# Linear attention and a GELU MLP on one core: the second weight cast by GpSimd's DMAs, and three changes of order

## The chip, the core and the metric

One core of a Trainium2 chip runs the whole program. The time is that of the device in microseconds, from a kernel that is launched once; smaller is better. Three runs of the kernel before took 264.68, 264.91 and 265.53 us.

The core has TensorE (PE in the profile; PEld is its loading of weights), VectorE (DVE), ScalarE (ACT), GpSimd (POOL), and SyncE (SP), which here only issues DMAs. Sixteen DMA engines move the data.

## What is computed

Eight batches, eight heads, 576 positions, 64 values per head, all in float32:

```python
q_s = exp(q - max(q, -1)); q_s /= sum(q_s, -1)        # over the 64 values
k_s = exp(k - max(k, 2));  k_s /= sum(k_s, 2)         # over the 576 positions
kv  = einsum('bhsd,bhse->bhde', k_s, v)
x   = einsum('bhsd,bhde->bhse', q_s, kv)              # to 4608 rows of 512
h   = x @ w_in                                        # 512 x 2048
g   = 0.5 * h * (1 + erf(h / sqrt(2)))
out = g @ w_out                                       # 2048 x 512
```

## The kernel before

The program is written in order by hand for each engine: an engine does its instructions in the order of the code, and semaphores make it wait for the others. Nothing is reordered behind the author's back.

**Chunks.** The 4608 rows are nine chunks of 512: chunk c (0 to 7) is the first 512 positions of batch c, and chunk 8 is the 64 left over of each batch. For a batch, ACT takes exponentials of q (`exp_q`) and k (`exp_k`), DVE sums q's over the 64 values (`q_sums`), DVE or GpSimd scales them (`q_scale`, `norm_q`), v is cast to bf16 (`cast_v`), PE makes k'v (`kv_mm`), DVE divides it (`kv_norm`). The scaled q is transposed: on PE for batches 0 and 1 (`tp_mm`, `tp_quarters`), by a transposing DMA from SP for the later ones (`xbar_step`). PE then makes x (`x_mm`), which DVE and ACT copy out of PSUM (`x_evac`).

**The two large products.** Chunk 0's are plain: `h_phase` does h in 16 tiles t of 128 hidden units, in groups, with GELU on ACT, and `y_mm` sums the 16 tiles into four banks. Chunk 1's h is plain too (`h_pairs`). From chunk 1's output product (`y_phase`) on, and from chunk 2's h (`h_waves`) on, the products are done in Strassen's way, with seven products of half size in place of eight. The seven are numbered 1 to 7 in the calls `mm(1, ...)` to `mm(7, ...)`, and each needs sums of operands: `quad_weights` makes those of w_in (four DVE operations for each of two sets, `sums0` and `sums`), `mix_wo` those of w_out (in `w16`, `w7` and in place), `x_sums` those of x, `s_parts` those of g (into `s5`, `s12` and in place). In `y_phase` the order is 1, 5, 6, 2, 7, 3, 4; bank `pa` takes products 1, 6, 7 and 4, where 6 and 7 are added onto what is there, so what is there must have been copied out first. `after(i)` calls what `ins` has for product i: the work of later batches that is to stand there in the engines' orders. `y_last` does chunk 8's output product in two halves j, each with three banks of its own, and stores each piece as it is done.

**Banks.** PSUM has eight banks. `roles` says which bank has which task in a chunk, and `turn_roles` permutes them from chunk to chunk. In `h_waves` the argument `mid` is set for chunk 2 alone, where the order of the wave is another one.

**Weights.** w_in comes by ten SP DMAs into float32 tiles `wi` (tags w0 to w4), in five blocks of 256, 256, 512, 512 and 512 columns. `cast_wi` and `cast_wi_dm` make bf16 of it in `wi_bf`, where a block of n columns is read with stride n/128: hidden unit m of tile c is column m n/128 + c. w_out comes by further SP DMAs (`load_wo`, `load_wo_row`) in the same order of rows, 4 or 8 KB in a row per partition, and DVE and ACT cast it (`cast_wo`) into `wo_bf`. On SP the loads stand in this order: q, k, v of batch 0, w_in, three quarters of w_out, then q, k and v of batch 1 with the rest of w_out between them, then batch 2 (`load(2)`). `wst` is the pool of those weight tiles; a tile of the same tag waits until the one before it is read: `quad_s` of `sums0` takes w4 and `w16` takes w0.

Of the kernel before, what the change touches and what calls it, by code (L numbers as in the profile page):

```python
# [8 lines left out]
FP32 = mybir.dt.float32  # L9
# [7 lines left out]
def kernel(  # L17
# [122 lines left out]
    def load(b):  # L140
        load_main(b, "q", q)
        load_pair(b, "k", k)
        load_pair(b, "v", v)
# [289 lines left out]

    def quad_weights(w):

        q = quad["s"][w] = wst.tile([128, 4, 2, 512], BF16, tag=("w4", "w1")[w], name="quad_s")
        up, dn = slice(w * 512, w * 512 + 512), slice((w + 2) * 512, (w + 3) * 512)
        a11, a12 = wi_bf[:, 0:2, up], wi_bf[:, 2:4, up]
        a21, a22 = wi_bf[:, 0:2, dn], wi_bf[:, 2:4, dn]
        s1, s2, s3, s4 = (q[:, i] for i in range(4))  # L440
        return [
            lambda: tt(s1, a21, a22), lambda: tt(s2, s1, a11, ALU.subtract),
            lambda: tt(s3, a11, a21, ALU.subtract), lambda: tt(s4, a12, s2, ALU.subtract),
        ]
# [13 lines left out]
    def turn_roles():  # L458

        r = dict(roles)  # L460
        roles.update(bb=r["x3"], ba=r["kv1"], x0=r["bb"], x1=r["kv0"], x2=r["x0"], x3=r["ba"],
                     kv0=r["x1"], kv1=r["x2"])

    def h_waves(c, mid):
# [144 lines left out]
        s_parts(c, 0, 4, (2, 3, 4) if mid else (3, 4))  # L609
        s_parts(c, 4, 4, (1, 2, 3, 4))  # L610
        turn_roles()

    def h_phase(c, ins, groups={}, banks={}, t1=0):

# [54 lines left out]
    def y_phase(c, ins):  # L669

        act, wgt = y_operands(c)
        at = {"ya": 2, "yb": 0, "yc": 3} if c == 1 else {"ya": roles["ba"], "yb": roles["bb"], "yc": roles["x0"]}
        pa, pb, pc = (bank(at[n], n) for n in ("ya", "yb", "yc"))
        ysb = [moe_sb.tile([128, 2, DM], FP32, tag="y_sb", name="y_sb", bufs=2) for i in range(2)]
        c11, c12 = ysb[0][:, :, 0:HN], ysb[0][:, :, HN:DM]
        c21, c22 = ysb[1][:, :, 0:HN], ysb[1][:, :, HN:DM]

        def two(ps):
            return ps.rearrange("p (j n) -> p j n", j=2)

        def mm(m, ps, first):
            for j in range(2):
                for k in range(HK):
                    nc.tensor.matmul(  # L684
                        ps[:, j * HN:(j + 1) * HN], act[m][:, k, j * 128:(j + 1) * 128],
                        wgt[m][:, k, :], start=(first and k == 0 and j == 0),
                        stop=(k == HK - 1), skip_group_check=True,
                    )

        def after(i):  # L690
            for fn in ins.get(i, []):
                fn()

        mm(1, pa, True)
        nc.scalar.copy(out=c11, in_=two(pa))  # L695
        after(1)
        mm(5, pb, True)
        nc.vector.tensor_copy(out=c22, in_=two(pb))
        after(5)
        mm(6, pa, False)  # L700
        tt(two(pb), two(pa), c22)
        after(6)
        mm(2, pc, True)
        tt(c11, c11, two(pc))
        after(2)
        mm(7, pa, False)
        tt(c22, two(pa), c22)
        after(7)
        mm(3, pb, False)
        nc.scalar.copy(out=c12, in_=two(pb))  # L710
        y_store(c, 0, ysb[0])
        after(3)
        mm(4, pa, False)
        nc.scalar.copy(out=c21, in_=two(pa))
        y_store(c, 1, ysb[1])
        after(4)

    def y_last(c):
# [16 lines left out]
        def mm(j, m, ps, first, n=slice(0, HN)):  # L735
            for k in range(HK):
                nc.tensor.matmul(  # L737
                    ps[:, n], act[m][:, k, j * 128:(j + 1) * 128], wgt[m][:, k, n],
                    start=(first and k == 0), stop=(k == HK - 1), skip_group_check=True,
                )  # L740

        for j in range(2):
            pa, pb, pc = banks[j]
            c11, c12 = ysb[0][:, j, 0:HN], ysb[0][:, j, HN:DM]
            c21, c22 = ysb[1][:, j, 0:HN], ysb[1][:, j, HN:DM]
            mm(j, 1, pa, True)
            nc.scalar.copy(out=c11, in_=pa)
            if j:
                store(0, 0, HN, both, (0,))
                store(1, 0, 0, both, (0,))  # L750
            mm(j, 5, pb, True)
            nc.scalar.copy(out=c22, in_=pb)
            mm(j, 6, pa, False)
            tt(pb, pa, c22)
# [35 lines left out]
        return w  # L790


    def cast_wi(i, w, eng):
        n = wi_cols[i]
        r = n // 128
        o = wi_bf[:, :, wi_off[i]:wi_off[i] + n].rearrange("p d (c m) -> p d c m", c=r)
        w = w[:, :, 0:n].rearrange("p d (m c) -> p d c m", c=r)
        if eng == "pv":

            nc.gpsimd.tensor_copy(out=o[:, 0:2], in_=w[:, 0:2])  # L800
            nc.vector.tensor_copy(out=o[:, 2:4], in_=w[:, 2:4])
        else:
            for c in range(NDM):
                nc.vector.tensor_copy(out=o[:, c], in_=w[:, c])  # L804

    def cast_wi_dm(i, w, dm, eng):

        n = wi_cols[i]
        r = n // 128
        o = wi_bf[:, dm, wi_off[i]:wi_off[i] + n].rearrange("p (c m) -> p c m", c=r)  # L810
        w = w[:, dm, 0:n].rearrange("p (m c) -> p c m", c=r)
        eng.tensor_copy(out=o, in_=w)

    def load_wo(i):
        w = wst.tile([128, 4, DM], FP32, tag=f"w{i}", name="w")
        src = moe_w_out[i * 512:(i + 1) * 512, :]
        if i == 0:
            for h in range(2):
                nc.sync.dma_start(
                    out=w[:, 2 * h:2 * h + 2],  # L820
                    in_=src[256 * h:256 * h + 256].rearrange("(p c) f -> p c f", c=2),
                )
            return w
        src = src.rearrange("(p c) f -> p c f", c=4)
        if i == 3:
            nc.sync.dma_start(out=w[:, 0:2], in_=src[:, 0:2])
            return w
        nc.sync.dma_start(out=w, in_=src)
        return w

    def load_wo_row(w, c):
        src = moe_w_out[3 * 512:4 * 512, :].rearrange("(p c) f -> p c f", c=4)
        nc.sync.dma_start(out=w[:, c], in_=src[:, c])

    def cast_wo(i, w, c0=0, n=4, eng="v"):
        o, w = wo_bf[:, 4 * i + c0:4 * i + c0 + n, :], w[:, c0:c0 + n]
        if eng == "v":
            nc.vector.tensor_copy(out=o, in_=w)
        else:
            nc.scalar.copy(out=o, in_=w)  # L840

    w16 = None

# [23 lines left out]


    touch = singles.tile([16, 3, 2], FP32)
    for i, a in enumerate((v[0].rearrange("h (p n) d -> (h p) (n d)", n=NS)[0:128:8, 0:2],  # L870
                           moe_w_in[0:128:8, 0:2], moe_w_out[0:512:32, 0:2])):
        nc.scalar.dma_start(out=touch[:, i, :], in_=a)

    load_pair(0, "v", v, 4)
    wi = [load_wi(i) for i in range(5)]
    wo = [load_wo(i) for i in range(3)]
    load_main(1, "q", q, 2)
    load_k1(0)
    wo.append(load_wo(3))
    load_k1(1)  # L880
    for hp in range(2):
        load_v1(hp)
    load_wo_row(wo[3], 2)
    load_wo_row(wo[3], 3)
    load_v1(2)
    load_v1(3)
    load(2)
    nc.vector.memset(zeros32, 0.0)
    setup_tiles()
    warm(7, zeros32)  # L890
# [20 lines left out]
    kv_mm(0, 1)  # L911
    kv_norm(0, 1)
    for dm in range(NDM):
        cast_wi_dm(0, wi[0], dm, nc.gpsimd)
    x_tile(0, 3, psum_h, "h")
    x_mm(0, 0)
    x_evac(0, 0, "s")
# [1 line left out]
    x_mm(0, 1)  # L919
    x_evac(0, 2, "s")  # L920
    x_evac(0, 3)
    cast_wi(1, wi[1], "pv")
    table(AF.Gelu)

    def ybank():
# [1 line left out]

    sums0 = quad_weights(0)
    h_phase(0, {
        0: [lambda: cast_wi(2, wi[2], "v")],  # L930
        2: [lambda: cast_wi(3, wi[3], "v")],
        6: [lambda: cast_wi(4, wi[4], "v")],
        9: sums0[0:2] + [lambda: cast_wo(0, wo[0])],
        15: [lambda: cast_wo(1, wo[1], eng="s")],
    }, groups={0: 2, 4: 4, 8: 4}, banks={
        3: ybank, 6: ybank, 8: ybank,
        9: lambda: psum_a.tile([128, M], FP32, tag="a", name="ps"),
# [3 lines left out]

    exp_q(1, parts=2)
    exp_k(1, parts=2, part=0)
    cast_wo(3, wo[3], 0, 1, "s")
    cast_wo(3, wo[3], 1, 1, "s")
    exp_k(1, parts=2, part=1)
    table(AF.Gelu)
    w16 = wst.tile([128, 2, HK, HN], BF16, tag="w0", name="w16")
    sums = quad_weights(1)
    for fn in sums0[2:]:  # L950
        fn()
    cast_wo(2, wo[2])
    for m in (3, 2, 4):
        mix_wo(m, 0)
    tps = [psum.tile([128, HP, J, 64], BF16, tag=f"k{i}", name="tp") for i in (5, 1)]
# [11 lines left out]
        y_part(t, range(J))  # L967
    load(3)
    mix_wo(1, 0)
    cast_wo(3, wo[3], 2, 1)  # L970
    cast_wo(3, wo[3], 3, 1)
    y_part(12, range(J))
    y_part(13, range(J))
    tp_quarters(1, tps)
# [37 lines left out]
    for m in (3, 2, 4, 1):  # L1012
# [1 line left out]
    quad["r"] = wst.tile([128, 4, 2, HT], FP32, tag="w2", name="r")  # L1014
    quad["t"] = wst.tile([128, 4, 2, HT], BF16, tag="w3", name="quad_t")
    h1 = {p + 3: [lambda p=p: cast_v(2, p, nc.scalar)] for p in range(HP)}
    h1[1] = [sums[0]]
    h1[3] += sums[1:3]
    h_pairs(1, h1, done=t1s, turn=Banks(2, 0, 5, 6))

# [3 lines left out]

    y_phase(1, {
        1: [sums[3], lambda: norm_q(2, 0, 2)],
        5: [lambda: norm_q(2, 1, 2, nc.vector)],
        6: [lambda: cast_v_all(3), lambda: xbar_step(2), lambda: exp_q(3)],
        2: [lambda: kv_step(2), lambda: exp_k(3), lambda: q_sums(3)],
        3: [lambda: table(AF.Gelu)],  # L1030
        4: [lambda: load(4), lambda: x_all(2, (3, 4, 1, 5)),
            lambda: kv_step(3, lambda: x_sums(2, (1,))), lambda: x_sums(2, (2,))],
# [73 lines left out]
```

## Time and profile before

| what | value |
|---|---|
| median of three runs | 264.91 us (264.68 to 265.53) |
| the profiled execution | 264.49 us, of which 262.4 us are its span, from first to last instruction |
| mean granted TensorE clock | 0.993 |
| bytes moved by DMA | 50.23 MB, mean 191 GB/s |
| ACT busy in the span | 190.1 us |
| DVE busy in the span | 190.0 us |
| POOL busy in the span | 54.5 us |

A line of a group or of the timeline names line, engine, operation and tiles (out<-in). Idle time stands with what ended it: `[3.26 <-ACT y_sb L695]` is 3.26 us in which the engine waited, ended by that copy on ACT. In a list of waits a line reads: who waited <- for whom: microseconds in total, times, the longest. A clock of 0.50 is half of the full TensorE clock.

### The profile page before, as it was taken

To read this page: it belongs to the slowest core of one execution; us is meant where nothing else is said; L and a number is where in the kernel's file an instruction comes from. 1 tells how busy PE (TensorE), PEld (TensorE's weight loads), DVE (VectorE), ACT (ScalarE), POOL (GpSimd) and SP (SyncE) were. 2 spreads that over 40 slices of the span, in tenths; PEclk is the share of its full clock that TensorE was granted. 3 is DMA by queue.
4 is the path that set the end of the run, shared out by engine and by line. 5 is a ranking of instruction groups with operands and counts; after the bars stand their busy time and mean duration, and the time that the engine had idled before them with its cause. 6 is when DMAs were issued, how large, how long until landed. Compare 5 with 4: busy or idle time off the path is not lost.

```text
span 262.4 us, 6525 instructions
## 1 busy us (share of the span) xinstructions
PE 251.1 (96%) x2678; PEld 196.9 (75%) x2678; DVE 190.0 (72%) x336; ACT 190.1 (72%) x324; POOL 54.5 (21%) x85
## 2 busy tenths in 40 slices
PE   7999999995999899999999999999999999999993
PEld 3544444444778788888888888888888888888783
DVE  1878699778468778687868886887688679548922
ACT  4876887799556986789688958895888587068721
POOL 1520033003404136004700470047000700000000
PEclk9999999999799999999999999999999999999999
DMA  7999999991319998880787079402700250040033
GB/s 241 400 381 424 402 406 399 397 418 61 82 80 319 327 308 315 204 318 1 260 231 273 6 258 223 99 2 78 166 4 0 82 160 2 0 162 2 0 80 84
DMA packets 43166, 50.23 MB, mean 191 GB/s; under 512 B 20224, under 2 KB 30464, under 8 KB 42880
## 3 DMA queue, kind: packets, MB, share of 16 engines
q1 hardware_dynamic: 42416, 49.13, 55.3%
q10 hardware_dynamic: 720, 0.69, 1.0%
q8 instruction: 21, 0.34, 0.6%
q14 instruction: 9, 0.07, 0.1%
HBM read 36.70 MB, written 9.44 MB: 176 GB/s over the span
## 4 chain that ended last, share of the span: by engine, by line
PE 73%; DMA 12%; ACT 7%; DVE 4%; issue 1%; POOL 1%; ACTq 1%; SPq 0%; DVEq 0%
PE ya L684 18%; PE qa L498 16%; PE yb L684 8%; PE qb L498 8%; DMA w<-in_moe_w_in_dram 6%; PE ps L387 5%; PE yc L684 5%; PE qc L498 4%; DMA f<-in_v_dram 4%; ACT g L522 3%; PE ya L737 2%; DMA touch<-in_moe_w_out_dram 2%; PE kv L225 2%; PE ps L353 2%; PE yb L737 1%
## 5 line engine op out<-in xcount | busy, mean ns | idle before, releaser
L684 PEld LDWEIGHTS <-g 128*128 128x128 bf16 x448 | 43.3, 98 | 7.9 <-issue 2.2
L498 PEld LDWEIGHTS <-quad_s 128*128 128x128 bf16 x448 | 43.8, 98 | 5.1
L684 PEld LDWEIGHTS <-s 128*128 128x128 bf16 x336 | 33.6, 100 | 7.9 <-issue 3.4
L498 PEld LDWEIGHTS <-wi_bf 128*128 128x128 bf16 x336 | 32.8, 98 | 3.8
L278 POOL TENSOR_TENSOR e<-e,recq 128x256 bf16<-128x256 bf16 x40 | 24.3, 644 | 31.3 <-DVE recq L264 21.0
L498 PE MATMUL qa<-quad_t,quad_s 128*128 128x256 bf16 x224 | 29.2, 273 | 0.0
L430 DVE TENSOR_TENSOR qb<-qa,r 128x512 f32<-128x512 f32 x28 | 18.2, 694 | 14.1 <-PE qa L498 9.6
L387 PE MATMUL ps<-xT,wi_bf 128*128 128x512 bf16 x128 | 28.2, 379 | 0.0
L684 PE MATMUL ya<-w,g 128*128 128x256 bf16 x224 | 26.8, 273 | 0.6 <-DVE y_sb L430 0.6
L684 PE MATMUL yb<-wo_bf,s 128*128 128x256 bf16 x224 | 26.7, 273 | 0.0
L263 DVE TENSOR_REDUCE qsum<-e 128x16 f32<-128x1024 bf16 (+1 forms) x12 | 20.9, 1738 | 5.6 <-ACT e L173 5.6
L387 PEld LDWEIGHTS <-wi_bf 128*128 128x128 bf16 x128 | 12.3, 98 | 15.3 <-DVE wi_bf L804 0.6
L393 ACT ACTIVATE g<-ps 128x512 bf16<-128x512 f32 x32 | 17.6, 601 | 6.2 <-PE ps L387 5.8
L173 ACT ACTIVATE e<-f 128x512 bf16<-128x512 f32 (+1 forms) x42 | 20.5, 557 | 1.9 <-DMA f<-in_q_dram 1.5
L522 ACT ACTIVATE g<-r 128x512 bf16<-128x512 f32 x28 | 17.3, 631 | 6.1 <-DVE r L430 6.1
L522 ACT ACTIVATE g<-qc 128x512 bf16<-128x512 f32 x28 | 15.2, 594 | 7.4 <-PE qc L498 7.4
L710 ACT COPY y_sb<-yb 128x512 f32<-128x512 f32 x7 | 4.1, 587 | 21.4 <-PE yb L684 21.4
L269 POOL TENSOR_TENSOR e<-e,recq 128x1024 bf16<-128x1024 bf16 (+1 forms) x4 | 9.3, 2332 | 48.8 <-DVE recq L264 48.8
L378 DVE CAST xT<-ps 128x512 bf16<-128x512 f32 x18 | 11.7, 687 | 10.0 <-PE ps L353 8.4
L430 DVE TENSOR_TENSOR r<-qa,r 128x512 f32<-128x512 f32 x28 | 18.0, 684 | 1.0 <-PE qa L498 0.7
L684 PE MATMUL ya<-w,s 128*128 128x256 bf16 x112 | 15.0, 292 | 3.3 <-ACT y_sb L695 3.3
L190 POOL CAST v_aug<-f 128x576 bf16<-128x576 f32 x25 | 17.5, 738 | 2.5 <-DMA f<-in_v_dram 2.4
(95 smaller groups left out, 447.9 us busy)
## 6 DMA issues: line engine op xcount, KB each, us to landing
out_dram<-y_sb SPq DMA_DIRECT2D x16, 512.0 KB, 3.7
f<-in_k_dram SPq DMA_DIRECT2D x6, 1152.0 KB, 9.9
f<-in_v_dram SPq DMA_DIRECT2D x6, 1152.0 KB, 9.2
f<-in_q_dram SPq DMA_DIRECT2D x6, 1024.0 KB, 7.2
w<-in_moe_w_in_dram SPq DMA_DIRECT2D x6, 512.0 KB, 9.2
f<-in_v_dram SPq DMA_DIRECT2D x8, 288.0 KB, 6.2
f<-in_q_dram SPq DMA_DIRECT2D x4, 512.0 KB, 8.9
w<-in_moe_w_out_dram SPq DMA_DIRECT2D x2, 1024.0 KB, 11.8
```

The lines of the kernel that those rows point to most:

```text
L173: nc.scalar.activation(out=dst[:, i], in_=src[:, u], func=AF.Exp)
L190: eng.tensor_copy(out=o, in_=i)
L263: nc.vector.reduce_sum(out=qsum, in_=st[b]["eq"][:, :, i * w:(i + 1) * w, :], axis=AX.X)
L269: eng.tensor_tensor(out=e, in0=e, in1=st[b]["recq"].unsqueeze(3).to_broadcast([128, J, w, D]), op=ALU.mult,)
L278: nc.gpsimd.tensor_tensor(out=e, in0=e, op=ALU.mult, in1=st[b]["recq"][:, j, i:i + 4].unsqueeze(2).to_broadcast([128, 4, D]),)
L378: nc.vector.tensor_copy(out=st[b]["xT"][:, hp, :], in_=ps)
L387: nc.tensor.matmul(ps, wi_bf[:, dm, t * 128:(t + 1) * 128], st[c]["xT"][:, dm, :], start=(dm == 0), stop=(dm == NDM - 1),)
L393: nc.scalar.activation(out=st[c]["g"][:, t, :], in_=ps, func=AF.Gelu)
L430: eng.tensor_tensor(out=out, in0=in0, in1=in1, op=op)
L498: nc.tensor.matmul(held[kind, q][:, u], w, mov[m][:, k], start=(m in (1, 5) and u == 0 and k == 0), stop=(k == 1), skip_group_check=True,)
L522: nc.scalar.activation(out=g[:, t:t + 2, half], in_=held[kind, q], func=AF.Gelu)
L684: nc.tensor.matmul(ps[:, j * HN:(j + 1) * HN], act[m][:, k, j * 128:(j + 1) * 128], wgt[m][:, k, :], start=(first and k == 0 and j == 0), ...
```

## The change

It does five things.

1. In chunk 1's `y_phase` the copy of product 1 is DVE's, not ACT's; the second half of q's norm for batch 2 stands after product 6's sum, not after product 5's copy; the sum over e of batch 3 stands after product 7's sum, not after `kv_step(2)`.
2. After chunk 2's wave two banks change places in `roles`.
3. `y_last` does product 1 of both halves first.
4. w_in's columns lie in plain order in `wi_bf`, and the casts read without a stride, four of a quarter and then two of a half for each block. The sums of w_in's sets (`sums0`, `sums`) move forward in DVE's order, and two weight tiles change tags.
5. w_out comes by four GpSimd DMAs, each of four tiles (512 rows of 2 KB), float32 in memory and bf16 in `wo_bf`; the casts on DVE and ACT go. GpSimd issues them after a copy of one column that waits for the first half of w_in's last block. SP issues a DMA of 16 values of `wo_bf` tile 7, which waits for the second of the four, and behind it the loads of batch 1 and 2.

```diff
@@ quad_weights
-        q = quad["s"][w] = wst.tile([128, 4, 2, 512], BF16, tag=("w4", "w1")[w], name="quad_s")
+        q = quad["s"][w] = wst.tile([128, 4, 2, 512], BF16, tag=("w0", "w1")[w], name="quad_s")
@@ h_waves
         turn_roles()
+        if mid:
+            roles.update(ba=roles["x2"], x2=roles["ba"])
@@ y_phase
-        nc.scalar.copy(out=c11, in_=two(pa))
+        (nc.vector.tensor_copy if c == 1 else nc.scalar.copy)(out=c11, in_=two(pa))
@@ y_last
         for j in range(2):
+            mm(j, 1, banks[j][0], True)
+            nc.scalar.copy(out=ysb[0][:, j, 0:HN], in_=banks[j][0])
+        for j in range(2):
...
-            mm(j, 1, pa, True)
-            nc.scalar.copy(out=c11, in_=pa)
+            mm(j, 5, pb, True)
             if j:
                 store(0, 0, HN, both, (0,))
                 store(1, 0, 0, both, (0,))
-            mm(j, 5, pb, True)
@@ weights
-    def cast_wi(i, w, eng):
...
-    def cast_wo(i, w, c0=0, n=4, eng="v"):
...
+    def cast_wi(i, w, eng, d0=0, n=1):
+
+        c = slice(wi_off[i], wi_off[i] + wi_cols[i])
+        eng.tensor_copy(out=wi_bf[:, d0:d0 + n, c], in_=w[:, d0:d0 + n, 0:wi_cols[i]])
+
+    def load_wo(t, n=4):
+
+        nc.gpsimd.dma_start(
+            out=wo_bf[:, t:t + n, :],
+            in_=moe_w_out[t * 128:(t + n) * 128, :].rearrange("(t p) f -> p t f", p=128),
+        )
@@ the start
+    landed = singles.tile([16, 2], BF16)
...
-    wo = [load_wo(i) for i in range(3)]
-    load_main(1, "q", q, 2)
-    load_k1(0)
-    wo.append(load_wo(3))
-    load_k1(1)
-    for hp in range(2):
-        load_v1(hp)
-    load_wo_row(wo[3], 2)
-    load_wo_row(wo[3], 3)
-    load_v1(2)
-    load_v1(3)
-    load(2)
...
-    cast_wi(1, wi[1], "pv")
+    cast_wi(1, wi[1], nc.gpsimd, 0, 2)
+    cast_wi(1, wi[1], nc.vector, 2, 2)
+    nc.gpsimd.tensor_copy(out=scr[:, 2:3], in_=wi[4][:, 0, 0:1])
+    for t in range(0, NDF, 4):
+        load_wo(t)
+    nc.sync.dma_start(out=landed[:, 0:1], in_=wo_bf[0:16, 7, 0:1])
+    load_main(1, "q", q, 2)
+    load_k1(0)
+    load_k1(1)
+    for hp in range(HP):
+        load_v1(hp)
+    load(2)
...
-        0: [lambda: cast_wi(2, wi[2], "v")],
-        2: [lambda: cast_wi(3, wi[3], "v")],
-        6: [lambda: cast_wi(4, wi[4], "v")],
-        9: sums0[0:2] + [lambda: cast_wo(0, wo[0])],
-        15: [lambda: cast_wo(1, wo[1], eng="s")],
+        0: [lambda d=d: cast_wi(2, wi[2], nc.vector, d) for d in range(NDM)],
+        2: [lambda d=d: cast_wi(3, wi[3], nc.vector, d, 2) for d in (0, 2)] + sums0[0:2],
+        6: [lambda d=d: cast_wi(4, wi[4], nc.vector, d, 2) for d in (0, 2)] + sums0[2:],
...
-    w16 = wst.tile([128, 2, HK, HN], BF16, tag="w0", name="w16")
+    w16 = wst.tile([128, 2, HK, HN], BF16, tag="w4", name="w16")
     sums = quad_weights(1)
-    for fn in sums0[2:]:
-        fn()
-    cast_wo(2, wo[2])
+    sums[0]()
...
-    h1[1] = [sums[0]]
...
-        5: [lambda: norm_q(2, 1, 2, nc.vector)],
-        6: [lambda: cast_v_all(3), lambda: xbar_step(2), lambda: exp_q(3)],
-        2: [lambda: kv_step(2), lambda: exp_k(3), lambda: q_sums(3)],
+        6: [lambda: norm_q(2, 1, 2, nc.vector), lambda: cast_v_all(3), lambda: xbar_step(2), lambda: exp_q(3)],
+        2: [lambda: kv_step(2), lambda: exp_k(3)],
+        7: [lambda: q_sums(3)],
```

## The prediction

> **What bounds the kernel now.** I read the page first, then the waits of PE, the order of time around each of them, and then the DMA views for the first 45 us, because that is where the change puts something new.
>
> ```profile
> span 262.4 us, 6525 instructions
> PE 251.1 (96%) x2678; PEld 196.9 (75%) x2678; DVE 190.0 (72%) x336; ACT 190.1 (72%) x324; POOL 54.5 (21%) x85
> ...
> PEclk9999999999799999999999999999999999999999
> DMA  7999999991319998880787079402700250040033
> ```
>
> PE is the bound: 11.3 us of the span are not PE. The clock has one dip, and the DMA engines are full from the start until about 60 us. The waits of PE tell what can be won:
>
> ```profile
> PE ya L684 <- ACT y_sb L695: 3.3, 1, 3.3
> ...
> PE ya L684 <- ACT g L522: 0.8, 1, 0.8
> PE ya L684 <- DVE y_sb L430: 0.6, 1, 0.6
> PE yb L737 <- ACT g L522: 0.6, 1, 0.6
> ```
>
> The timeline shows the first and the third of them, both in the output product of chunk 1 (start, length, engine, what):
>
> ```profile
> 62.49 2.11 ACT L178 ACTIVATE ek<-f 128x2304 bf16<-128x2304 f32 x1
> ...
> 64.50 0.56 ACT L695 COPY y_sb<-ya 128x512 f32<-128x512 f32 x1
> ...
> 65.12 3.50 PE L684 MATMUL ya<-w,s 128*128 128x256 bf16 x16 [3.26 <-ACT y_sb L695]
> 66.36 1.74 SPq L333 DMA_TRANSPOSE qT<-e  x1
> ...
> 72.06 2.27 DVE L263 TENSOR_REDUCE qsum<-e 128x32 f32<-128x2048 bf16 x1
> ...
> 75.39 1.91 PE L684 MATMUL ya<-w,g 128*128 128x256 bf16 x16 [0.59 <-DVE y_sb L430]
> ...
> 77.22 0.63 PE L353 MATMUL ps<-qT,kvc 64*64 64x512 bf16 x8
> ```
>
> The copy of the first product (L695) stands on ACT behind a table load and seven exponentials, so PE stops for 3.26 us; then 16 products take 3.50 us instead of 1.75. In the table by stretches (length, busy PE, PEld, DVE, ACT, POOL, clock, DMA) the second stretch has half the clock:
>
> ```profile
> 61.80:65.20 3.40, 0.14 (x2) 0.08 (x1) 3.30 (x6) 3.40 (x6) 2.04 (x2) 1.00 0.00 0
> 65.20:68.60 3.40, 3.40 (x17) 2.35 (x17) 1.00 (x1) 3.40 (x5) 3.36 (x4) 0.50 0.34 77
> ```
>
> For the start, from the timeline:
>
> ```profile
> 35.70 4.26 PE L633 MATMUL ps<-wo_bf,g 128*128 128x512 bf16 x19
> ...
> 37.35 1.73 DVE L269 TENSOR_TENSOR e<-e,recq 128x1024 bf16<-128x1024 bf16 x1
> ...
> 38.69 1.99 POOL L190 CAST v_aug<-f 128x576 bf16<-128x576 f32 x2 [0.69 <-DMA f<-in_v_dram]
> ...
> 39.89 0.71 PE L317 MATMUL tp<-identity,e 64*64 64x64 bf16 x64
> ```
>
> and from the DMA view what the 16 engines moved from 12 to 34 us (plain loads), and from 67.6 to 69.7 us (the transposing DMA alone):
>
> ```profile
> DMA packets 4320, 8.86 MB, mean 403 GB/s; under 512 B 271, under 2 KB 1962, under 8 KB 4063
> ```
>
> ```profile
> DMA packets 2080, 0.52 MB, mean 250 GB/s; under 512 B 2080, under 2 KB 2080, under 8 KB 2080
> ```
>
> PE has hardly a gap from 13.8 to 61.9 us, but only just: chunk 0's output product (L633) starts at 27.71, q of batch 1 is scaled at 39.08, v's first two pieces are cast at 40.68, and the transposes start at 39.89, kv at 40.42.
>
> **Chunk 1's product.** The first copy goes to DVE (0.63 to 0.69 us, rows of L698), ahead of quad_s and of the sum over e, so it runs at 60.1 to 60.8 while PE still does the second product, and the third can start at 61.7. (The buffer it writes must have been stored: before, that store landed at 60.25. The copy of c22 behind it on DVE comes at 62.95, as before at 62.91.) PE then goes on at 1.75 us a product: mm(6) 61.7, mm(2) 63.45, kv 65.2 (0.7), mm(7) 65.9, mm(3) 67.65, mm(4) 69.4, x 71.15. Now the moved steps. The second half of q's norm stands behind the sum into yb: 64.4 to 67.4 on DVE (1.20 + 0.25 + 1.23 to 1.73), so the transposing DMA is issued at 67.4 instead of 66.36 and lands 3.8 us later, 71.2: next to PE's 71.15. Behind that on DVE: the sum of c11 (0.65), kvc (0.9), then the sum of c22, done at 69.65, so mm(4) waits 0.25. The sum over e of batch 3 (2.28 + 0.35) now comes after it, so the 0.59 wait is gone, but the evacuation of x waits for DVE until 72.3; ACT, with five exponentials, a table load and two copies to do first, is free at the same time. The next wave starts at 73.05 instead of 78.50: **5.45 us**, of them 3.26 wait, 1.75 clock.
>
> **Chunk 2.** The swap of two banks gives product 1 a bank whose gelu ended earlier; the wait of 0.83 goes. Next late: s5's second half is ready at 93.18 and then needed at 93.1, so I take **0.7**. **Last chunk:** eight more products (0.87) stand ahead of the one that waited 0.55 for a gelu: **0.55**. The two ACT stores that move by one product cost nothing: the tail hangs on PE.
>
> **w_in in plain order.** Twelve strided DVE casts of 0.62 become four of at most 0.62 and four of 128x1024 at 0.6 to 0.7 (rows of 128x2048 at 1.22 and 128x1024 at 0.69). With w_out's casts (DVE 3.7 us, ACT 3.0) that is some 5 us of DVE work less in a stretch where PE runs anyway: nothing. If a contiguous cast gained nothing, PE's need for the last w_in block at 24.4 would still find it within 0.3 us.
>
> **w_out by GpSimd.** SP's loads of w_out go (4.19 MB), and on SP q, k and v of batch 1, and behind them all loads of batch 2, now stand behind the small DMA that waits for w_out's second piece; ACT's exponentials, GpSimd's casts of v and then PE wait for those. GpSimd waits for the first half of w_in's last block, issued at 12.97, landed at 22.40 (the trace has issue and landing of each DMA). Behind that wait stand its scaling of q and casts of v, not due before 36; it is idle from 15.1 to 36, which hides its descriptors as long as they take less than 13 us. First bytes: 22.7 plus the 1.3 us that the transposing DMA took from issue to first packet, 24.0; SP's queue is dry at 22.0, so 2 us are lost. No row shows a casting DMA. Bounds: 403 to 410 GB/s of source bytes (w_in's 2 KB rows reach it), and 250 GB/s, the only row where a DMA changes what it moves. I take 410, since size and shape are those of w_in. Then piece 0 ends at 26.6 and lands at 28.2 (landings trail last bytes by 1.6: 20.7 and 22.4 for that w_in block), 0.5 late for PE's 27.71; piece 1 lands at 30.8, piece 2 at 33.3, piece 3 at 37.5, in time. SP issues q at 31.3, first bytes at 32.6, shared with pieces 2 and 3 until 35.9. q's halves land at 36.8 and 38.4 (before: 32.4, 33.8), k at 39.9 and 41.3, v at 42.1 to 44.2 (before: 38.6 to 42.1). From q's second half: exponentials 1.35, sum 1.2 + 0.25, scale 1.73: 43.0 against 39.89. Two v casts on GpSimd, 0.67 to 1.0 each, end at 43.9 against the 43.65 where kv wants them. PE loses **3.3 us** there (the 0.5 is inside it). The first store's buffer lands at 62.2 and is wanted at 63.4: no wait; v of batch 2 lands at 52.6 (50.55 before) and ACT wants it at 55.2 (51.9 before).
>
> The Trainium skill (DMA: Bandwidth & Descriptors, "Anatomy of one DMA") fits a GpSimd DMA as 2.0 us plus bytes at 436 GB/s; as an estimate piece 0 would land at 27.1 instead of 28.2, and the sum below would be 1.1 smaller. No run here shows it.
>
> **Sum.** 262.4 - 5.45 - 0.7 - 0.55 + 3.3 = 259.0. The profiled run took 264.49, 2.1 more than its span, and lies 0.4 under the median, so 259.0 + 2.5 = **261.5** on the median's scale.
>
> **Rivals.**
> *Casting DMAs are slow (slower).* At 250 GB/s the 4.19 MB take 16.8 us instead of 10.2; batch 1 queues behind and beside them, so PE loses 3.3 + 6.6 = 9.9 and the time is 268.1. It decides where w_out costs 3.4 us more than I think, 13.6 us or 308 GB/s. For it: the 250 GB/s row, smaller writes, descriptors made by GpSimd. Against: w_in's rate with the same rows.
>
> *DVE holds up GpSimd's descriptors.* GpSimd's cast of v takes 1.0 beside a two-input DVE operation (38.69, two in 1.99) and 0.67 alone (41.42). Between 22.7 and 26.8 DVE has two casts and four sums of 0.69, one of them half done. Two held casts cost 1.4, the whole stretch 4.1: 262.9 to 265.6. The skill (SBUF — State Buffer, "Who interferes with whom") says that a two-port DVE cast shuts GpSimd out for its whole length and that two-input sums leave descriptor writing alone; by that rule it is 262.9. The 1.0 against 0.67 agrees that they share something.
>
> *Chunk 1's wait comes back as qT.* If the transposing DMA queues behind batch 3's loads, which end 2 us later than before (about 61), or DVE runs late, x starts 2 us later: 263.5. Against: the DMA views show nothing in flight from 61 to 67.
>
> *The start is cheaper.* Half the bytes are written, and if the 2 us gap closes, PE loses 1.3: 259.5.
>
> PE's idle 2.5 us near 41 is under the 3.26 that halved the clock; if it does so again, 1.75 more.
>
> **Chances.** Forecast 0.42 (its own range 259.5 to 264), slow casts 0.32, DVE holds descriptors 0.12, qT 0.06, cheaper start 0.08. A measurement of this kernel can tell about 0.3%, 0.8 us. Faster: 0.41 + 0.07 + 0.05 + 0.08 = 0.61; same 0.06; slower 0.33. The range runs from below the cheap start, 258.9, to above the slow casts, 268.6.
>
> **What would show it.** Right: no PE wait at the copy of ya in chunk 1, clock 1.0 there, x of batch 2 some 13 us after that product's start; w_out's pieces 2.6 us apart, the first landing near 28; PE idle 2.5 to 3.5 us before the transposes of batch 1. Wrong: pieces 4 us apart or GpSimd busy for many us per DMA, PE waiting on wo_bf more than once, or the wait of chunk 1 moved onto the qT load.

## The result, and the profile after

The changed kernel takes 265.74 us (median of 20 runs, 264.94 to 266.31), the kernel before 264.50 in the same series. The ratio is 1.0054, with a 95% interval of 1.0033 to 1.0074: slower by half a per cent, where 261.5 us, a faster kernel, was forecast. The gains of the three changes of order came as forecast. The start lost 9.08 us where 3.3 were forecast.

The page of the profiled execution after, which took 266.11 us:

```profile
span 264.3 us, 6516 instructions
PE 250.9 (95%) x2678; PEld 196.2 (74%) x2678; DVE 184.3 (70%) x329; ACT 186.8 (71%) x320; POOL 57.8 (22%) x90
...
PEclk9999999599999999999999999999999999999999
DMA  7996999999029999893579258901700260021034
```

Each digit is a slice of 6.6 us. The dip of the clock has moved from the eleventh slice (near 65 us) to the eighth (46 to 53 us) and is deeper. The DMA row has a 6 in its fourth slice (20 to 26 us) where a 9 stood before. The waits of PE after:

```profile
PE tp L317 <- POOL e L269: 2.6, 1, 2.6
PE tp L317 <- ACT ek L178: 1.9, 1, 1.9
...
PE kv L225 <- POOL v_aug L190: 1.1, 2, 0.8
```

All four waits shown of before are gone, 3.3 us at the copy of ya among them. In their place PE waits for batch 1: for its scaled q (L269, and again in the second line: ACT's ek ends at 46.35 only by coincidence; the second half of q's scaling on DVE ends at 46.22, and in the experiment with an earlier start of GpSimd the same transposes begin 0.41 us before that ek ends and, as here, 0.15 after the scaling), then for v (L190). The timeline of chunk 1's product after:

```profile
67.18 2.01 PE L686 MATMUL ya<-wo_bf,g 128*128 128x256 bf16 x16
...
69.23 0.69 DVE L697 COPY y_sb<-ya 128x512 f32<-128x512 f32 x1 [0.20 <-PE ya L686]
...
70.78 1.91 PE L686 MATMUL ya<-w,s 128*128 128x256 bf16 x16
...
81.06 0.63 PE L353 MATMUL ps<-qT,kvc 64*64 64x512 bf16 x8 [0.52 <-DMA qT<-e]
...
82.31 1.92 PE L498 MATMUL qa<-xT,wi_bf 128*128 128x256 bf16 x16
```

The copy runs on DVE beside the second product, the third starts 3.60 us after the first, and each takes 1.75 us to the next. From the first product to the next wave it is 15.13 us instead of 20.40. But the whole stands 9.08 us later than before (67.18 against 58.10). Where these go is in the timeline of the start:

```profile
29.20 12.25 PE L635 MATMUL ps<-wo_bf,g 128*128 128x512 bf16 x56 [0.50 <-DMA wo_bf<-in_moe_w_out_dram]
44.03 0.45 PE L317 MATMUL tp<-identity,e 64*64 64x64 bf16 x32 [2.58 <-POOL e L269]
46.37 0.64 PE L317 MATMUL tp<-identity,e 64*64 64x64 bf16 x32 [1.89 <-ACT ek L178]
...
47.87 0.70 PE L225 MATMUL kv<-v_aug,ek 64*64 64x65 bf16 x34 [0.80 <-POOL v_aug L190]
48.50 3.17 PE L635 MATMUL ps<-wo_bf,g 128*128 128x512 bf16 x7
```

Chunk 0's output product starts 1.49 us later (29.20 against 27.71). Only 0.50 of it is the wait for w_out; chunk 0's hidden layer itself ends 0.99 later, having started 0.37 later (14.20 against 13.83) and waited 0.19 for a cast of w_in. (In the three runs below with SP's loads of w_out that product starts, without a wait, at 27.68 to 28.23.) The transposes of batch 1 start another 2.65 later (44.03 against 39.89, so 4.14 in all). Between the halves of the transposes and before kv PE waits 1.89 and 0.80 more. Then seven products take 3.17 us where they took 1.68; the half clock, with the small steps and seams around these products, makes the rest, 2.25. The sum is 1.49 + 2.65 + 2.69 + 2.25 = 9.08.

In stretches (length, busy PE, PEld, DVE, ACT, POOL, clock, DMA share, GB/s; a share above 1 sums packets that overlap), the DMAs before the waits and the clock beside them:

```profile
22.80:26.00 3.20, 3.01 (x15) 1.05 (x13) 3.10 (x6) 1.84 (x4) 2.89 (x5) 1.00 0.38 23
```

```profile
42.14:45.55 3.41, 0.45 (x32) 0.34 (x32) 2.03 (x3) 2.77 (x5) 1.84 (x1) 1.00 1.06 391
45.55:48.96 3.41, 1.79 (x70) 1.34 (x71) 2.73 (x7) 3.38 (x5) 2.46 (x3) 0.50 1.09 358
48.96:52.37 3.41, 3.41 (x35) 1.23 (x37) 0.90 (x4) 1.05 (x3) 0.00 (x0) 0.50 1.05 388
```

For 3.2 us, from 22.8 to 26.0, next to nothing is moved (23 GB/s): w_in is done but for its last packets, which end at 23.94, and w_out has hardly begun. The clock stands at half for 6.83 us, twice the time of before.

By the trace of DMAs, GpSimd issues its four from 23.23 to 26.49 and they land at 29.16, 32.48, 35.02 and 37.75. The small DMA is issued at 32.49; q lands at 39.13 and 42.16 (before: 32.42 and 33.80), v's four pieces from 45.91 to 48.19 (before: 38.64 to 42.09). A landing is counted in sixteen steps in the trace: q's second half has fifteen of them by 40.55, and the last is 1.61 behind.

### The profile page after: what moved, and what is told of

It reads as the page before. It is cut to its first block, busy times and chain, and to the rows that moved or that the text cites. A ratio compares the mean times of both kernels' runs of the same rounds, so it can differ in the third digit from the quotient of the medians.

```text
span 264.3 us, 6516 instructions
## 1 busy us (share of the span) xinstructions
PE 250.9 (95%) x2678; PEld 196.2 (74%) x2678; DVE 184.3 (70%) x329; ACT 186.8 (71%) x320; POOL 57.8 (22%) x90
## 4 chain that ended last, share of the span: by engine, by line
PE 74%; DMA 17%; POOL 2%; DVE 2%; issue 2%; SPq 1%; ACT 1%; ACTq 0%; POOLq 0%
PE qa L498 18%; PE ya L686 15%; PE qb L498 9%; PE yb L686 8%; DMA w<-in_moe_w_in_dram 6%; PE ps L387 5%; PE qc L498 5%; DMA f<-in_v_dram 4%; PE yc L686 4%; DMA wo_bf<-in_moe_w_out_dram 3%; PE ya L739 2%; DMA touch<-in_moe_w_in_dram 2%; PE kv L225 2%; DMA qT<-e 2%; POOL v_aug L190 2%; PE ps L353 2%
## 5 line engine op out<-in xcount | busy, mean ns | idle before, releaser
L686 PEld LDWEIGHTS <-s 128*128 128x128 bf16 x336 | 32.8, 98 | 4.2 <-DVE s L430 0.4
L498 PEld LDWEIGHTS <-wi_bf 128*128 128x128 bf16 x336 | 32.8, 98 | 3.8
L269 POOL TENSOR_TENSOR e<-e,recq 128x1024 bf16<-128x1024 bf16 (+1 forms) x4 | 9.3, 2330 | 46.2 <-DVE recq L264 39.4
L190 POOL CAST v_aug<-f 128x576 bf16<-128x576 f32 x25 | 17.3, 727 | 3.4 <-DMA f<-in_v_dram 3.3
L178 ACT ACTIVATE ek<-f 128x2304 bf16<-128x2304 f32 (+1 forms) x10 | 17.2, 1728 | 0.6 <-DMA f<-in_k_dram 0.6
L635 PE MATMUL ps<-wo_bf,g 128*128 128x512 bf16 x64 | 15.8, 407 | 0.5 <-DMA wo_bf<-in_moe_w_out_dram 0.5
```

What stands on the lines that cost most here:

```text
L178: nc.scalar.activation(out=ek[b % 2][:, i:i + n], in_=st[b]["kf"][:, i:i + n].rearrange("p x (n d) -> p x n d", n=NS), func=AF.Exp,)
L190: eng.tensor_copy(out=o, in_=i)
L498: nc.tensor.matmul(held[kind, q][:, u], w, mov[m][:, k], start=(m in (1, 5) and u == 0 and k == 0), stop=(k == 1), skip_group_check=True,)
L635: nc.tensor.matmul(ps, st[c]["g"][:, t, j * 128:(j + 1) * 128], wo_bf[:, t, :], start=(t == 0), stop=(t == NDF - 1),)
L686: nc.tensor.matmul(ps[:, j * HN:(j + 1) * HN], act[m][:, k, j * 128:(j + 1) * 128], wgt[m][:, k, :], start=(first and k == 0 and j == 0), ...
```

## The experiments

**The orders alone.** The kernel before with changes 1 to 3; weights loaded as before.

```diff
-        nc.scalar.copy(out=c11, in_=two(pa))
+        (nc.vector.tensor_copy if c == 1 else nc.scalar.copy)(out=c11, in_=two(pa))
...
-        5: [lambda: norm_q(2, 1, 2, nc.vector)],
-        6: [lambda: cast_v_all(3), lambda: xbar_step(2), lambda: exp_q(3)],
-        2: [lambda: kv_step(2), lambda: exp_k(3), lambda: q_sums(3)],
+        6: [lambda: norm_q(2, 1, 2, nc.vector), lambda: cast_v_all(3), lambda: xbar_step(2), lambda: exp_q(3)],
+        2: [lambda: kv_step(2), lambda: exp_k(3)],
+        7: [lambda: q_sums(3)],
```

> The kernel before with the three changes of order alone (chunk 1's first copy on DVE and its norm and sum later, the bank swap in chunk 2, the two first products of the last chunk together); w_in and w_out are loaded and cast as before. Theory A, the orders gain what the trace shows and the whole loss is at the start: product of chunk 1 to next wave in 15.1 us instead of 20.4, first wait of chunk 2's product gone, so about 6.5 us less than before, 258.0. Rival, part of that gain comes from the new loading (the late loads keep the DMA engines and buffers out of the way, DVE is freer): 260 or more, with waits left in chunk 1's product.

Measured: 257.61 us, ratio 0.9741 (0.9727 to 0.9756). From the first product of chunk 1 to the next wave it is 14.80 us. The waits of PE in this kernel, all of them:

```profile
PE ps L865 <- DVE scr L90: 1.5, 1, 1.5
PE ps L353 <- DVE kvc L238: 0.3, 1, 0.3
PE qa L498 <- ACT xT L380: 0.2, 1, 0.2
```

Beyond the 1.5 us of the start-up PE waits half a microsecond in all. So the orders are worth some 6.9 us by themselves, and what the changed kernel has beyond them costs 265.7 - 257.6 = 8.1. A second run of this kernel, beside the next one, for which was expected:

> The kernel with the three changes of order alone once more, beside the one with plain rows on the same chip: 257.6, a ratio to the kernel before of 0.974.

Measured: 257.66 us, ratio 0.9755 (0.9727 to 0.9783).

**The plain order of rows and columns, without GpSimd's DMAs.** The orders, and w_in and w_out in plain order, loaded by SP.

```diff
-        src = src.rearrange("(p c) f -> p c f", c=4)
+        src = src.rearrange("(c p) f -> p c f", p=128)
...
-        o = wi_bf[:, :, wi_off[i]:wi_off[i] + n].rearrange("p d (c m) -> p d c m", c=r)
-        w = w[:, :, 0:n].rearrange("p d (m c) -> p d c m", c=r)
...
+        c = slice(wi_off[i], wi_off[i] + wi_cols[i])
+        eng.tensor_copy(out=wi_bf[:, d0:d0 + n, c], in_=w[:, d0:d0 + n, 0:wi_cols[i]])
```

> The kernel with the three changes of order (257.6 before), and w_in's columns and w_out's rows in plain order, still loaded by SP as they were and cast by DVE and ACT. It parts the plain order from the loading by GpSimd. Theory A, the plain order costs nothing and frees DVE only where nobody waits for it: 257.6, within 0.4. Rivals: the contiguous casts bring chunk 0's hidden layer forward, 256.5 to 257.2; or w_out's rows in packets of 2 KB instead of up to 8 KB make its loads slower and the output product of chunk 0 waits, 258.3 to 259.5.

Measured: 257.55 us, against 257.66 for the orders alone on the same chip. Plain order costs nothing and brings nothing. So the 8.1 us belong to w_out's way through GpSimd's DMAs and to what stands behind it. (The sums of weights stand here where they stood before; their new place is tried below, without effect.)

**No small DMA in front of batch 1.** Its loads follow w_in's on SP at once.

```diff
-    nc.sync.dma_start(out=landed[:, 0:1], in_=wo_bf[0:16, 7, 0:1])
     load_main(1, "q", q, 2)
```

> The changed kernel without the small DMA that waits for w_out's second piece: batch 1's and 2's loads stand on SP right behind w_in's. Theory A, SP's queue is served only where GpSimd's has nothing to move: q of batch 1 fills the gap from 22.8 to 26 us and lands by 27, then SP's queue moves nothing until GpSimd's has ended near 36.5; k lands near 39, v from 40 to 42; PE loses about 2.5 us before chunk 1 instead of 9 and the time is about 260. Rival B, the queues share and it was the small DMA that plugged SP's queue: both queues move bytes from 26 us on, w_out's pieces land 4 to 5 us apart instead of 2.5 to 3.3, PE waits for w_out two or three times, and the time is 266 to 272.

Measured: 268.36 us, ratio 1.0127 (1.0096 to 1.0158). My first theory fell. The queues of DMA from 34 to 41 us in this kernel (packets, MB, time of the packets as a share of 16 engines):

```profile
q0 software_dynamic: 851, 0.86, 71.7%
q1 hardware_dynamic: 850, 0.88, 45.0%
```

GpSimd's queue (q0) and SP's (q1) take turns packet by packet: 851 and 850. So they do share. A packet of GpSimd's takes 1.6 times as long, and each packet of 1 KB bf16 stands for 2 KB of w_out. The pieces of w_out land at 33.14, 38.34, 42.65 and 48.74, and PE waits for three of them (4.9, 0.7 and 2.5 us). In this kernel GpSimd's first bytes move only at 27.05, 3.3 us after the end of the first issue; SP's queue was full.

**The small DMA behind the first piece, not the second.** That parts "nothing until the other queue has drained" from "late by a fixed line, then shared".

```diff
-    nc.sync.dma_start(out=landed[:, 0:1], in_=wo_bf[0:16, 7, 0:1])
+    nc.sync.dma_start(out=landed[:, 0:1], in_=wo_bf[0:16, 3, 0:1])
```

> The changed kernel with the small DMA waiting for w_out's first piece instead of its second, so SP issues it near 29.2 us, 3.3 earlier, while GpSimd's queue has work until 37 or later. In the changed kernel SP's first bytes came 3.3 us after the end of that issue and at the moment GpSimd's queue drained; the two are told apart here. Theory A1, a queue that has run dry gets nothing until the other one has drained: first bytes at 36.4 again, q lands at 39 and 42, time 265 to 266. Theory A2, a queue that starts beside a busy one gets its first bytes some 3.3 us after the issue and then shares with it: first bytes near 33, q lands near 36.5 and 39, w_out's last piece near 40, PE idle 2 to 3 us less before the transposes, time 262 to 263.5.

Measured: 265.82 us, ratio 1.0064 (1.0036 to 1.0092). The first bytes came as theory A2 has it, and then the queues share: from 29.6 to 32.8 us, and from 34 to 38:

```profile
q0 software_dynamic: 637, 0.64, 120.6%
```

```profile
q0 software_dynamic: 493, 0.49, 72.2%
q1 hardware_dynamic: 495, 0.49, 44.6%
```

SP's issue ends at 29.57 and its first packets run at 32.88, 3.3 us later; then the two share. Landings and time did not follow: q lands at 38.42 and 42.12, where A2 had 36.5 and 39 and the changed kernel 39.13 and 42.16, and w_out's last piece at 39.69 instead of 37.75. What q gained at the front w_out lost. The late first packet is real, but is not what the 8 us are made of: whatever the order of the bytes, q's second half comes after all of w_out.

**q of batch 1 ahead of the small DMA.** It fills the stretch in which nothing moved.

```diff
-    nc.sync.dma_start(out=landed[:, 0:1], in_=wo_bf[0:16, 7, 0:1])
     load_main(1, "q", q, 2)
+    nc.sync.dma_start(out=landed[:, 0:1], in_=wo_bf[0:16, 7, 0:1])
     load_k1(0)
```

> The changed kernel with the two loads of q of batch 1 ahead of the small DMA that waits for w_out's second piece, k and v behind it as they were. Both theories: q lands near 25.5 and 27 us, so the transposes of batch 1 no longer wait, and only kv does. Theory A (SP's queue stands while GpSimd's has work): k starts at 36.4 and lands near 39.5 and 41, v from 41.7 to 44; PE idle about 2 us in all near 42 instead of 5.3, one window of the clock or none at half, time 259 to 260.5. Rival B (they share once the small DMA has landed): k's first bytes at 33, k lands near 36 and 38, v from 39 to 41, PE not idle there, time near 258.

Measured: 261.33 us, ratio 0.9876 (0.9856 to 0.9896), 4.4 us less than the changed kernel. The transposes follow the product without a wait at 42.09, kv waits 0.70 and 0.55, and the clock stays whole. k's first bytes come at 36.2, when GpSimd's queue runs out, and the time lies above both expectations. The first piece of w_out lands at 29.86, and PE waits 1.26 for it.

**An earlier start of GpSimd.** Its first DMA waits for the first half of w_in's block 3.

```diff
-    nc.gpsimd.tensor_copy(out=scr[:, 2:3], in_=wi[4][:, 0, 0:1])
+    nc.gpsimd.tensor_copy(out=scr[:, 2:3], in_=wi[3][:, 0, 0:1])
```

> The changed kernel with GpSimd's first w_out DMA waiting for the first half of w_in's block 3 (landed 20.4) instead of block 4 (23.05). Theory A with the gap as part of the loss: the four DMAs are issued from 20.5 to 23.8, first bytes at 22.2, full rate at 23.4; the pieces land near 26.5, 29.8, 32.3 and 35, q starts at 33.7, PE loses about 6.3 us at the start instead of 9, time about 263; the last half of w_in lands up to 1 us later if GpSimd's queue goes before SP's. Rival, the slow first bytes (24.9 to 26) come from what DVE does at 23.9 to 27 us (casts and sums) and not from the queue's start: the pieces still reach full rate only after DVE's sums, later than 25, and the time is 264.5 or more.

Measured: 262.89 us, ratio 0.9934 (0.9916 to 0.9952), 2.9 less than the changed kernel and what the theory of the gap gives. GpSimd issues from 20.90 on and the last piece lands at 35.63; q's second half lands at 38.41, 3.75 earlier. That is more than the 2.33 us by which GpSimd's issue moved: the fifteenth of the landing's sixteen steps is 2.44 earlier (38.11 against 40.55), and the last follows 0.30 behind it instead of 1.61. Full rate is reached at 24.0, while DVE still casts.

**Both edits together.**

> The changed kernel with q of batch 1 ahead of the small DMA and GpSimd's start on the first half of w_in's block 3, that is, the two edits that brought 4.4 and 2.9 us, together. Theory A2 (a new queue beside a busy one waits some 3.3 us from the end of its issue, then shares): GpSimd issues at 20.9, its first bytes come near 25, as in the kernel with q ahead alone, so the early start brings little: 260.5 to 261.3. Rival, the gains add up because the queue starts as soon as it is issued: first bytes at 22.5, shared with q, k about 2 us earlier, 258.5 to 259.5.

Measured: 259.88 us, ratio 0.9839 (0.9798 to 0.9879), 5.9 less than the changed kernel; between the two expectations. GpSimd's first bytes move at 25.27, 3.1 us after the end of the first issue, as A2 has it; but SP's loads of q run out at the same moment (343 GB/s near 24.6 us, 35 near 25.6), so this run does not tell the two apart. From 26 to 35 us w_out then moves without a dip:

```profile
26.00:35.00 9.00, 7.66 (x36) 3.41 (x35) 1.35 (x3) 6.32 (x12) 0.00 (x0) 1.00 1.24 207
```

What is left against the orders alone is 2.2 us: PE waits 1.34 for the first piece (landed 30.10) and 0.54 for v. Fifteen of the sixteen steps of that piece's landing are there at 28.59, before PE wants it at 28.80; the last one is the wait.

**PE kept busy where it waited.** Eleven products ahead of batch 1's transposes and eight between their halves; nobody reads their results.

```diff
+    def fill(i, n):
+        ps = bank(i, "fill")
+        for _ in range(n):
+            nc.tensor.matmul(ps, identity, wo_bf[:, 12, :], start=True, stop=True)
+
+    fill(5, 11)
...
-    tp_quarters(1, tps)
+    tp_quarters(1, tps, lambda: fill(6, 8))
```

> The changed kernel with 11 products of 128x512 ahead of batch 1's transposes and 8 more between their halves, whose results nobody reads; they take 2.4 and 1.7 us, just under the two idle stretches of PE (2.58 and 1.89). Theory A, PE's idle time halves the clock and the half clock costs 1.7 us by itself: the clock stays 1.0 throughout, the products behind kv take 1.7 us instead of 3.2, and the time is 264.0. Rival, the half clock has another cause than the idle time: it comes again for 6.8 us and the time is 265.7 or a little more.

Measured: 264.23 us, ratio 0.9989 (0.9968 to 1.0011), 1.5 less than the changed kernel. The clock is whole throughout, and PE's timeline shows the products behind kv at full speed:

```profile
41.02 2.54 PE L936 MATMUL fill<-wo_bf,identity 128*128 128x512 bf16 x11
...
48.12 1.46 PE L637 MATMUL ps<-wo_bf,g 128*128 128x512 bf16 x6 [0.16 <-issue]
```

The half clock costs 1.5 us by itself by the medians and 1.7 by the ratios, and it comes from PE's idle time. The kernel before shows its price too: of its 31 executions beside this run, five with a mean clock of 1.0 took 262.4 to 263.0 us, and fourteen with 0.993, which is one stretch of 3.41 us at half, took 264.0 to 264.7.

**DVE out of GpSimd's way.** The four sums of weights move behind chunk 0's hidden layer.

```diff
-        2: [lambda d=d: cast_wi(3, wi[3], nc.vector, d, 2) for d in (0, 2)] + sums0[0:2],
-        6: [lambda d=d: cast_wi(4, wi[4], nc.vector, d, 2) for d in (0, 2)] + sums0[2:],
+        2: [lambda d=d: cast_wi(3, wi[3], nc.vector, d, 2) for d in (0, 2)],
+        6: [lambda d=d: cast_wi(4, wi[4], nc.vector, d, 2) for d in (0, 2)],
+        15: sums0,
```

> The changed kernel with DVE's four sums of weights (0.69 us each, at 22.5 to 27.3 us) moved behind chunk 0's hidden layer, so that beside GpSimd's four DMA issues DVE has only the two casts of w_in's last block. Rival (DVE holds up GpSimd's descriptors): GpSimd's four issues get shorter than 0.93, 0.80, 0.80 and 0.75, full rate comes before 26.0, the first piece lands 0.5 to 1 us earlier, and so do q and everything behind it: 264.7 to 265.2. Theory A (DVE has no part in it): issues and landings within 0.2 us of the changed kernel's, time 265.5 to 266.

Measured: 265.98 us, ratio 1.0062 (1.0041 to 1.0084). In the timeline of POOL the four issues take 3.21 us, 3.26 in the changed kernel:

```profile
23.18 0.71 POOL L879 COPY scr<-w 128x1 f32<-128x1 f32 x1 [7.02 <-DMA w<-in_moe_w_in_dram]
23.83 3.21 POOL L803 DMA_DIRECT2D wo_bf<-in_moe_w_out_dram  x4
```

The first piece lands 5.76 us after its issue (5.93 in the changed kernel). DVE's sums have no part in the slow start that could be measured.

**The first piece alone, the rest after the sums.**

```diff
     nc.gpsimd.tensor_copy(out=scr[:, 2:3], in_=wi[4][:, 0, 0:1])
-    for t in range(0, NDF, 4):
-        load_wo(t)
+    load_wo(0)
...
+    def rest():
+        nc.gpsimd.tensor_copy(out=scr[:, 2:3], in_=quad["s"][0][:, 3, 0, 0:1])
+        for t in range(4, NDF, 4):
+            load_wo(t)
```

> The changed kernel with only w_out's first piece issued by GpSimd where it was (23.2 us), and the other three, and SP's loads behind them, after DVE's last sum of weights near 27 us. Theory A3, the slow first bytes (24.9 to 26.0) come from GpSimd still writing descriptors for the later pieces: the first piece moves at full rate from 24.9 and lands at 28.0 to 28.3 instead of 29.16. Rival, the start of this queue is slow by itself: full rate again only from 26.0, landing at 29. In both the other pieces come later (issue from 27.2, landings near 32, 34.5 and 37.5 to 38.5) and the time is 266 to 268.

Measured: 266.32 us, ratio 1.0089 (1.0058 to 1.0120). The piece lands at 29.12, 5.83 after its issue; full rate comes at 26.2. Theory A3 fell: the queue starts as slowly with one DMA in it as with four.

## Why the prediction was wrong, and where it was right

**Right: the orders.** Chunk 1's product gained 5.27 us (20.40 to 15.13) for 5.45 forecast, with its parts as told: no wait at the copy, clock 1.0. The one step that ran over is x, 13.88 us after the product's start instead of 13.05, 0.52 of it waiting for qT. That is what the rival on qT has, at a quarter of its price, but not by its causes: DVE ends q's norm 9.25 us after the product's start, 9.3 as forecast, and batch 3's loads have landed by 66.14. The transposing DMA lands 4.42 us after its issue, and 3.71 to 3.73 in the three runs with SP's loads of w_out, where x starts at 13.29; why is open. Chunk 2's wait of 0.83 went (from wave to output product 13.24 became 12.26), and so did the 0.55 of the last chunk. Forecast together 6.7; the orders alone brought 6.5 to 6.9 by their ratios.

**Right: plain w_in, and the rate of a casting DMA.** Nothing was forecast for w_in, nothing came. The pieces of w_out land 3.3, 2.5 and 2.7 us apart, 2.6 forecast; 200 GB/s are written, that is 400 GB/s of float32 read. The rival of slow casting DMAs is refuted, and so is the one on DVE's hold of descriptors: the issues beside DVE's two casts took 0.80 us each, the one beside sums alone 0.75, which is 0.1 in place of the 1.4 that two held casts were to cost. That this rival's upper time, 265.6 us, lies next to the measured one is a coincidence. The rule cited from the Trainium skill (SBUF — State Buffer, "Who interferes with whom") shows in another instruction: GpSimd's copy of one column takes 0.19 us in the changed kernel and 0.71 beside a DVE cast (line above). For the descriptors no run shows it.

**Wrong: the term of 3.3 us at the start, which measured 9.08.** Three steps of it failed, and 0.99 us of the 9.08 stand ahead of them, in chunk 0's hidden layer. The 0.5 us for the first piece came out at 0.50 by luck: the piece landed at 29.16 instead of 28.2, and PE wanted it 0.99 later too.

1. "First bytes ... 24.0 ... so 2 us are lost." Full rate came at 26.0. The trigger landed 0.65 later in this execution; the rest, 1.3 us, is a queue that after its first packet at 24.87 stays slow for a microsecond. I had priced GpSimd's start by the first packet of another DMA, and not by the time to full rate. w_out's bytes then ended near 37 where the forecast's start and rate give 34.2 for them alone (24.0 plus 4.19 MB at 410 GB/s): 2.0 from the start, 0.8 from a dip to 139 GB/s written from 28.0 to 29.6 and 191 behind it.
2. "q's halves land at 36.8 and 38.4 ..." The second landed at 42.16, 2.8 because of w_out's end as just told and 0.9 more for q's own bytes and landing. Half of the 0.9 is the last of the landing's steps, 1.61 behind the fifteenth; the w_in block from which the prediction took its 1.6 between last byte and landing has it 1.11 behind. q's sharing with pieces 2 and 3 was not the point, as the small DMA behind piece 0 shows: shared or not, q's end stands behind w_out's. What follows from q was sized rightly: 4.6 us from q's landing to the second transposes forecast, 4.2 measured. The same 3.8 to 4 us then stand in v, and with v in kv. Putting q where the gap was won back 4.4 us of time, the earlier start 2.9, both 5.9 of the 8.1.
3. "PE's idle 2.5 us ... under the 3.26 that halved the clock." It was not one stretch of 2.5 but three, of 2.58, 1.89 and 0.80, close together, and the clock stood at half for 6.83 us. What counted was not the length of one gap but how little PE did in a stretch of 3.41 us, as told below. Filling PE gave 1.5 us back. The 1.75 that stood beside the sum as a possibility belonged into it, since a term of several us of idle PE brings it along.

A 3.76 us error in one landing thus made most of a 5.8 us error in time: about 2.5 in waits, 2.25 behind them, most of it the clock, and 1.0 in the hidden layer ahead of them, whose cause no run parts.

The faster kernel is the one with the orders alone: 257.6 us, against 264.5 before and 265.7 after.

## What to carry to other kernels

Before moving loads to another queue, look whether the DMA engines are already full in that stretch: here they were from the start to 60 us, so a queue that begins 3 us late pushes every later load by those 3 us, and casts saved on engines that nobody waits for pay nothing back. In a full stretch place the loads by when their users need them (q has a chain of 4 us behind it, so it goes first), and keep the old queue fed while the new one starts. Price idle PE together with the half clock that follows, by what PE does in each 3.41 us, and part a bundle of edits early: the orders alone were the gain, and the loading ate it.

## What the runs showed of the hardware that was not expected

- A queue that starts beside a full one is late by up to 3.4 us. From the end of the issue to the first packet it is 3.3 us without the small DMA (GpSimd beside SP) and 3.3 with the small DMA behind piece 0 (SP beside GpSimd), where the other queue stays full. Where the other queue runs out, the first packet comes at about that moment: after 3.3 us in the changed kernel, 3.4 with the first piece alone, 3.1 (GpSimd) and 2.1 (SP) with both edits, 1.1 and 2.4 with q ahead, 0.7 with the early start. It is 0.7 too where the other queue had run out already (24.16 to 24.87). It looks as if a new queue stood behind the descriptors that the other has already in line; that was not tried by itself. Once both run they take turns packet by packet (851 to 850). The Trainium skill (DMA: Bandwidth & Descriptors, "SWDGE vs HWDGE vs iDMA") says that an engine goes round robin between its queues; the trace agrees once both run, and not in the first 3 us.
- GpSimd's queue is at full rate 1.8 to 2.1 us after the end of its first issue in seven runs, 1.0 to 1.3 of it after its first packet: with one DMA in it or with four, whatever DVE does, on empty engines or where SP's loads just run out. With both edits, issued 3.1 us before its first packet, it is at full rate 0.3 after that packet. Why stays open, and so does the dip at the end of its first piece, which was absent with both edits.
- The clock halves after a stretch of 3.41 us in which PE worked a little, not only after an idle one: PE was busy 0.45 us of it in the changed kernel, 0.15 before, and the half lasted on over a stretch with 1.79. With the earlier start a stretch with PE busy 1.78 of 3.41 us (42.35 to 45.76, most of it small products) came ahead of a half clock. In the thirteen traces, counted in steps of 3.41 us from the first whole clock on, PE is busy 0.00 to 1.79 us in twelve stretches, and each is followed by a half clock; in all others that start before 250 us it is busy 1.93 or more, and none is. The Trainium skill (TensorE: Matmul & The Clock Gate, "Part 1: The HAM clock gate") has the clock fall after an idle window of some 3.4 us; the length agrees, that the window must be idle does not.
- After a load of instructions the last of a landing's sixteen steps lags. In the changed kernel a packet of 16 KB in the instruction queue (q8) takes 1.12 us from 39.61. The landing before it, of q's first half, has its last step 0.04 us behind the fifteenth; q's second half has it 1.61 behind, and k and v keep that distance. Behind the load near 16.6 us (16.4 before) w_in's landings show the same, among them the one that GpSimd's start waits for (21.71 and 23.05; before, 21.29 and 22.40). It looks as if one of the sixteen DMA engines were set back by the load; the trace does not name the engine of a packet, and no run takes the load away.
